# Batch 0's keys in chunks of 128 rows, with one value load each, in an attention and MLP kernel on one core

## The chip, the core and the metric

The kernel runs on one core of a Trainium2 chip. The metric is the device time of one execution in microseconds (us); less is better. Engines: PE (TensorE, matmuls), PEld (its weight loads), DVE (VectorE), ACT (ScalarE), POOL (GpSimd) and SP (SyncE). POOL and SP also issue DMAs.

## The reference

Eight batches, eight heads, 576 positions, head dimension 64; then an MLP on the 4608 tokens, 512 to 2048 to 512.

```python
q_d, k_d, v_d = (means over 4 neighbouring positions of q, k, v)
out_up = repeat(softmax(q_d k_d^T / 8) v_d, 4)            # downsampled attention, 144 x 144
mask = abs(pos[:, None] - pos[None, :]) < 4               # local attention: 7 keys a query
out_local = softmax(where(mask, q k^T / 8, -1e9)) v
x = (out_up + out_local) as [4608, 512]                   # heads side by side
h = x @ w_in
out = (h / (1 + exp(-1.702 h))) @ w_out
```

## The kernel before

The order on each engine is written out by hand: every engine runs its instructions in the order of the program text, and waits where it needs another engine's result. The kernel has a start, in which batch 0's attention is computed, and then nine groups `g` of 512 tokens, each with the two MLP matmuls (`mm1` with `hps_mm`, L764, and `mm2`, L845). The attention of batch `g + 1` is woven into group `g`'s matmuls at fixed places (`POS`, `POS_0`, `VDP_0`).

Local attention: the 576 queries are cut into five chunks `i` at a stride of 114. Before the change a chunk's keys are two runs of 64 (`KSTART`, at 114 i and 114 i + 56) on partitions 0 to 63 and 64 to 127, and each run serves 60 queries (`QSTART`, at 114 i and 114 i + 60). The runs overlap by 8 keys. For batches after the first, `exp_local` and `mask_local` cut out the band with the 0/1 tile `mask`. For batch 0 the band is kept in another way: `bar_others` (L372) first writes -1e6 or 0 into the PSUM tile from `off`, the scores (`scores`, L390) are added, and after the exponential (`exp_apart`, L454) all keys outside the band are zero. It writes to the tiles `ez`, which have 128 columns for each chunk and head; columns that no score reaches are filled once by `fill` (L125, L130, L133). Then `av_local0` (L474) makes one matmul for each chunk and head, with the exponentials as weights and the value tile `vbs[0]` (65 columns, the last one ones, which gives the denominator) as the moving side.

Downsampled attention: the sums of four values are made on PE by `prep_vd_pe` (L355), with a 0/1 selector `psel`, and copied to `vds` by ACT (L362). `scores_d` (L435) and `exp_down` (L461) make the downsampled exponentials `ed`, and `av_down0` (L487) multiplies them with `vds`. `normalise0` (L504 reciprocal, L505 product, DVE) divides both by their denominators into `y`; it is called with chunks 0 to 4 and 4 to 7 for head pairs 0 and 1, and for all seven slots for pairs 2 and 3. `turned` then makes 11 matmuls (`transp_sum`, L525) that turn `y` over and add both kinds, and `copy_x` copies the result to `xT` in three pieces (L536 to L538; ACT, for the last pair partly DVE). The MLP's first matmuls, `part`, read `xT` and `w_in_bf`.

The constants come from iotas on POOL: `dm` (key minus query, for `off` and `mask`), `di` (identity `id128`), `dr` (row number) and `dp` (for `psel`). DVE and ACT turn them into `off`, `id128`, `up` (identity with every column four times), `psel` and `mask` (`make_mask`: ACT's cast L146).

Loads of q, k, v for batches 0 and 1 and of the weights are issued by POOL, with a cast to bf16 on the way: k and q in head groups of four (`load_1`, L201), values as two loads of 64 rows for each chunk (`load_vb`, L232, ten loads a batch), `w_in` in pieces of columns (L255), `w_out` in four pieces (L264). Each POOL load takes the semaphore of the load eight places earlier and so waits until that one has landed. The issue order of the start is:

```python
load_qk(0, 0); load_1("k", k, kf, 0, 1); iota_mask(); load_1("q", q, qf, 0, 1); iota_psel()
fill()
for i in range(5): load_vb(0, i)
load_w_in(0, 512); load_w_in(512, 512); load_w_in(1024, 1024)
```

Dummy matmuls on zeros, `warm`, stand at places where PE would be idle.

Of the kernel before, what the change touches and what calls it, by code (L numbers as in the profile page):

```python
# [8 lines left out]
FP32 = mybir.dt.float32  # L9
# [10 lines left out]
def kernel(  # L20
# [20 lines left out]
    QSTART = (0, 60)  # L41

# [41 lines left out]
    off = consts.tile([128, 60], BF16, name="off")  # L84
    psel = consts.tile([128, 7, 64], BF16, name="psel")
    up = consts.tile([128, 128, 4], BF16, name="up")

    PSEL = [(4, 2), (2, 1), (0, 0), (1, 0), (1, 1), (3, 1), (3, 2)]

    dm = consts.tile([128, 60], FP32, name="dm")  # L90
    di = consts.tile([128, 128], FP32, name="di")
    dr = consts.tile([128, 1], FP32, name="dr")
    bias = consts.tile([128, 4], FP32, name="bias")
    dp = consts.tile([128, 7, 64], FP32, name="dp")
# [3 lines left out]
    def iota_psel():  # L98
        for par in range(2):
            nc.gpsimd.iota(dp[halves[par], 0:3], pattern=[[-72, 3], [-8, 64]],  # L100
                           base=2 * (KSTART[par] + 72) - 3, channel_multiplier=2, **it)
            nc.gpsimd.iota(dp[halves[par], 3:7], pattern=[[72, 2], [-384, 2], [-8, 64]],
                           base=2 * (KSTART[par] + 114) - 3, channel_multiplier=2, **it)

    def iota_mask():
        for par in range(2):
            nc.gpsimd.iota(dm[halves[par]], pattern=[[-1, 60]], base=-4 * par,
                           channel_multiplier=1, **it)
        nc.gpsimd.iota(dr, pattern=[[0, 1]], base=0, channel_multiplier=1, **it)
        nc.gpsimd.iota(di, pattern=[[-1, 128]], base=0, channel_multiplier=1, **it)  # L110

    def fill():
        nc.vector.memset(wz, 0.0)
        nc.vector.memset(ones[:, 0], 1.0)
        nc.vector.memset(ones[:, 1], 4.0)
        for t in kdT:
            nc.vector.memset(t[:, SD:160, :], 0.0)
        for t in vbs:
            nc.vector.memset(t[:, :, :, 64:65], 1.0)
        for t in vds:  # L120
            nc.vector.memset(t[:, :, :, 64:65], 4.0)
        for t in es:
            nc.vector.memset(t[:, :, 300:304], 1.0)
        for t in ez:
            nc.vector.memset(t.rearrange("p j i (x c) -> p (j i x) c", c=64)[:, :, 60:64], 1.0)  # L125
        for n, t in enumerate(ez):
            for par in range(2):
                rest = t[halves[par], :, :, 64 - 64 * par : 124 - 64 * par]
                if n < 2:
                    nc.vector.memset(rest, 0.0)  # L130
                else:
                    zero = wz[halves[par], None, 0:300].to_broadcast([64, 2, 300])
                    nc.scalar.copy(  # L133
                        out=rest, in_=zero.rearrange("p j (i c) -> p j i c", c=60)
                    )


    def make_off():
        nc.vector.tensor_tensor(out=dm, in0=dm, in1=dm, op=ALU.mult)
        nc.vector.tensor_single_scalar(out=dm, in_=dm, scalar=9.5, op=ALU.is_lt)  # L140
        nc.vector.tensor_scalar(
            out=off, in0=dm, scalar1=-1.0, scalar2=1e6, op0=ALU.add, op1=ALU.mult
        )

    def make_mask():
        nc.scalar.copy(  # L146
            out=mask.rearrange("p x (i c) -> p (x i) c", c=60),
            in_=dm[:, None, :].to_broadcast([128, 10, 60]),
        )

    def ident(pos, n, c0, c1):
        return id128[64 * pos : 64 * pos + n, 64 * pos + c0 : 64 * pos + c1]

# [3 lines left out]
    def make_bias():  # L157
        nc.vector.memset(bias[:, 3:4], -3.0)
        nc.vector.tensor_copy(out=bias[:, 0:2], in_=rv)
        nc.vector.tensor_scalar(  # L160
            out=bias[:, 0:2], in0=bias[:, 0:2], scalar1=-1.0, scalar2=400.0,
            op0=ALU.add, op1=ALU.mult,
        )
# [8 lines left out]
    def make_psel():  # L172
        nc.vector.tensor_single_scalar(
            out=rv, in_=dr.to_broadcast([128, 2]), scalar=57.5, op=ALU.is_lt
        )
        nc.vector.tensor_single_scalar(
            out=r2, in_=dr.to_broadcast([128, 2]), scalar=65.5, op=ALU.is_gt
        )
        nc.vector.scalar_tensor_tensor(
            out=r2[:, 0:1], in0=dr, scalar=121.5, in1=r2[:, 0:1],  # L180
            op0=ALU.is_lt, op1=ALU.mult,
        )
        nc.vector.tensor_tensor(out=rv, in0=rv, in1=r2, op=ALU.add)

    def end_psel():
        nc.scalar.activation(out=dp, in_=dp, func=AF.Abs)
        nc.scalar.activation(out=dp, in_=dp, func=AF.Relu, bias=bias[:, 3:4])
        for sl, c in ((slice(0, 1), 1), (slice(1, 7), 0)):
            nc.scalar.activation(
                out=psel[:, sl], in_=dp[:, sl],  # L190
                func=AF.Exp, scale=-400.0, bias=bias[:, c : c + 1],
            )

# [46 lines left out]

    def load_v4(b):
        for kc in range(3):
            for hp in range(HP):
                u, m = hp % 2, hp // 2
                nc.sync.dma_start(
                    out=v4[64 * u : 64 * u + 48, kc, 2 * m : 2 * m + 2],
                    in_=bass.AP(
                        tensor=v.tensor,
                        offset=v[b, 2 * hp].offset + kc * 48 * 4 * D,
                        ap=[[4 * D, 48], [S * D, 2], [1, 4 * D]],  # L250
                    ),
                )
# [21 lines left out]

    def prep_1(name, b, qd):
        store, dst = {"k": (kf, kT), "q": (qf, qT)}[name]
        tt = work.tile([128, S, 2], BF16, name=f"{name}T{qd}", tag=f"{name}T{qd}", bufs=1)
        t32 = tt.rearrange("p t a -> p (t a)").bitcast(FP32)
        nc.vector.transpose(  # L279
            out=t32.rearrange("p (i c) -> p c i", c=18),  # L280
            in_=store[b, qd].bitcast(FP32).rearrange("p (c d) -> p c d", c=18),
        )
        dst[b, qd] = tt
# [10 lines left out]
    def reduce_qk(b, qd, name):  # L294
        t = kdT[qd][:, 0:SD, :] if name == "k" else new_qdT(b, qd)
        src = (kT if name == "k" else qT)[b, qd]
        with nc.allow_low_precision("the sum is rounded once, as the pairwise one is"):
            nc.vector.tensor_reduce(
                out=t, in_=src.rearrange("p (j f) a -> p j a f", f=4),
                axis=mybir.AxisListType.X, op=ALU.add,  # L300
            )

    def pool_qk(b, qd, names="kq"):
        for name, src in (("k", kT), ("q", qT)):
            if name not in names:
                continue
            sv = src[b, qd].rearrange("p (j f) a -> p j f a", f=4)
# [31 lines left out]
    def prep_vd_pe(b, pv, kcs=range(3), between=None):  # L339
        vb, vd = vbs[b % 2], vds[b % 2]  # L340
# [6 lines left out]
        for kc, iis in ((0, (0, 1)), (1, (1, 2, 3)), (2, (3, 4))):  # L347
# [3 lines left out]
            for i in iis:  # L351
                if between:
                    between(kc, i)
                for j in range(2):
                    nc.tensor.matmul(  # L355
                        pv[64 * j : 64 * j + 64, c0 : c0 + D * HP],
                        lhsT=psel[:, PSEL.index((i, kc)), :],
# [12 lines left out]
    def bar_others(sp):  # L370
        for r in range(4):
            nc.tensor.matmul(  # L372
                sp[r // 2][:, r % 2, 0:300],
                lhsT=id128,
                rhs=off[:, None, :].to_broadcast([128, 5, 60]),
# [4 lines left out]
    def scores(b, qd, barred=False, sp=None):  # L380
        if barred:
            bar_others(sp)
        for i in range(5):
            for a in range(2):
                for par in range(2):
                    for r in range(4):
                        rows = slice(32 * r, 32 * r + 32)
                        k0 = 114 * i + KSTART[par]
                        q0 = 114 * i + QSTART[par]
                        nc.tensor.matmul(  # L390
                            sp[r // 2][64 * par : 64 * par + 64, r % 2, 60 * i : 60 * i + 60],
                            lhsT=kT[b, qd][rows, k0 : k0 + 64, a],
                            rhs=qT[b, qd][rows, q0 : q0 + 60, a],
                            start=(a == 0 and not barred),
                            stop=(a == 1 or barred),
                            tile_position=(32 * r, 64 * par),
                            skip_group_check=barred,
# [53 lines left out]
    def exp_apart(qd, sp):  # L451
        for u in range(2):
            for par in range(2):
                nc.scalar.activation(  # L454
                    out=ez[2 * qd + u][halves[par], :, :, 64 * par : 64 * par + 60],
                    in_=sp[u][halves[par], :, 0:300].rearrange("p j (i c) -> p j i c", c=60),
# [53 lines left out]
    def transp_sum(y, x):  # L510
# [9 lines left out]
            (128, i, x[i // 2 % 2][:, c + 3 : c + 117], sub(id128, 3, (61, 2), (1, 57)))  # L520
            for i, c in enumerate((0, 114, 0, 114, 228))
        ]
        turns += [(128, 4, x[0][:, 345:348], id128[:, 121:124])]
# [360 lines left out]
    load_qk(0, 0)  # L884
    load_1("k", k, kf, 0, 1)
    iota_mask()
# [3 lines left out]
    for i in range(5):  # L890
        load_vb(0, i)
    load_w_in(0, 512)
# [6 lines left out]
    warm(14)  # L899
    make_off()  # L900
    make_ident(di)
    make_up()
    make_psel()
    make_bias()
    end_psel()
    prep_1("k", 0, 0)
    prep_1("q", 0, 0)
    sp = scores(0, 0, barred=True, sp=PA[0:2])
# [9 lines left out]
    sp = scores(0, 1, barred=True, sp=PA[0:2])  # L918
    exp_apart(1, sp)
    warm(4, 256)  # L920
    for hp in range(4):
        o[hp] = PB[hp % 3]
        y[hp] = y_tiles0()
    prep_vd_pe(
        0, PM[0], range(0, 2),
        between=lambda kc, i: warm(2 * ((kc, i) == (1, 3)), t=PM[1]),
    )
    for hp in range(2):
        av_local0(hp, o[hp], range(4))
        normalise0(o[hp], y[hp], 0, 4)  # L930
    sd = scores_d(0, 1, PB[2])
    prep_vd_pe(0, PM[1], range(2, 3))
    exp_down(1, sd)
# [5 lines left out]
    make_mask()  # L939

# [16 lines left out]
    normalise0(o[3], y[3])  # L957
    turned(0, None)
# [13 lines left out]
    for g in range(n_groups):  # L972
        b = g + 1
        if g == 0:
# [4 lines left out]
            for qd in range(NQ):  # L979
# [3 lines left out]
                load_qk(2, qd)  # L983
            nc.gpsimd.memset(v4[32:64], 0.0)
# [57 lines left out]
```

## Time and profile before

| | |
|---|---|
| median of 3 runs | 314.41 us (314.29 to 315.14) |
| profiled execution | 316.73 us, its span 314.9 us, granted clock 0.998 |
| PE busy | 300.2 us (95%), 4266 matmuls |
| ACT, DVE, POOL busy | 208.5, 148.3, 151.0 us |
| chain that ended last | PE 86%, DVE 4%, ACT 3%, POOL 2%, DMA 2% |
| first MLP matmul (L764) | at 23.90 us |
| batch 1's value sums (L355) | at 46.58 us |

PE's share of the chain says that the span is the time of PE's work and of what holds it up. Times of single instructions are microseconds from the span's start. Busy PE time is of pipelined matmuls and is not a measure of peak.

### The profile page before, as it was taken

What the parts mean: (1) busy time and instruction counts of PE and PEld (TensorE: products, weight loads), DVE (VectorE), ACT (ScalarE), POOL (GpSimd) and SP (SyncE); (2) the same over time, 40 slices, a digit from 0 to 9 for tenths busy, and PEclk for the clock granted to TensorE, in tenths of its full rate; (3) what the DMA queues carried; (4) which work ended last, traced back from release to release, by engine and by line L of the source; (5) the groups of instructions that cost most, each with busy time, mean ns of one, the idle gap of its engine ahead of it and who ended that gap; (6) DMA issues with size and microseconds to landing.
All of it is one profiled execution on the core that took longest, in us unless ns stands there. A gap on an engine that the chain in (4) does not pass through costs nothing.

```text
span 314.9 us, 9860 instructions
## 1 busy us (share of the span) xinstructions
PE 300.2 (95%) x4266; PEld 161.2 (51%) x4308; DVE 148.3 (47%) x302; ACT 208.5 (66%) x332; POOL 151.0 (48%) x174
## 2 busy tenths in 40 slices
PE   7689999999999999999999999999999999999995
PEld 3467667745554455455545554555455544444444
DVE  7972925790497049803890289027922670000000
ACT  8664875686886688558955895589568857316611
POOL 8852374376336963597339833992397120000000
PEclk9999999999999999999999999999999999999999
DMA  7999999999916980699159914992430110011011
GB/s 120 117 190 211 187 88 194 183 251 232 199 70 173 193 175 36 186 184 200 40 158 191 200 60 134 194 203 76 128 95 5 67 69 0 33 67 35 0 67 67
DMA packets 64123, 39.96 MB, mean 127 GB/s; under 512 B 44624, under 2 KB 54992, under 8 KB 64080
## 3 DMA queue, kind: packets, MB, share of 16 engines
q0 software_dynamic: 18864, 14.95, 35.1%
q1 hardware_dynamic: 45072, 24.32, 30.2%
q8 instruction: 33, 0.54, 0.7%
q14 instruction: 10, 0.08, 0.1%
q10 hardware_dynamic: 144, 0.07, 0.1%
HBM read 44.83 MB, written 9.44 MB: 172 GB/s over the span
## 4 chain that ended last, share of the span: by engine, by line
PE 86%; DVE 4%; ACT 3%; POOL 2%; issue 2%; DMA 2%; DVEq 0%; POOLq 0%; ACTq 0%
PE pm L845 34%; PE pm L764 24%; PE pa L764 15%; PE pa L408 3%; PE pa L654 2%; DMA vb<-in_v_dram 2%; PE pa L632 2%; PE pa L435 2%; DVE y L505 1%; PE pm L860 1%; POOL vb L232 1%; ACT l L600 1%; DVE xT L607 1%; ACT l L589 1%; PE pa L845 1%
## 5 line engine op out<-in xcount | busy, mean ns | idle before, releaser
L845 PE MATMUL pm<-w_out_bf,gT 128*128 128x512 bf16 (+1 forms) x527 | 115.0, 371 | 3.2 <-issue 3.0
L764 PEld LDWEIGHTS <-w_in_bf 128*128 128x128 bf16 x614 | 59.3, 98 | 63.1 <-issue 1.0
L764 PE MATMUL pm<-xT,w_in_bf 128*128 128x512 bf16 (+1 forms) x351 | 87.0, 371 | 0.9 <-ACT osb L828 0.4
L845 PEld LDWEIGHTS <-gT 128*128 128x128 bf16 x604 | 56.9, 98 | 59.7 <-issue 0.7
L775 ACT ACTIVATE gT<-pm 128x512 bf16<-128x512 f32 x88 | 52.7, 604 | 41.0 <-PE pm L764 41.0
L764 PE MATMUL pa<-xT,w_in_bf 128*128 128x512 bf16 (+1 forms) x247 | 59.0, 359 | 0.4
L469 DVE TENSOR_TENSOR es<-es,mask 128x600 bf16<-128x600 bf16 x28 | 17.3, 652 | 88.1 <-ACT es L446 87.9
L828 ACT ACTIVATE osb<-pm 128x512 f32<-128x512 f32 (+2 forms) x35 | 20.3, 582 | 30.5 <-PE pm L845 25.1
L775 ACT ACTIVATE gT<-pa 128x512 bf16<-128x512 f32 x56 | 32.1, 610 | 6.4 <-PE pa L764 6.3
L724 POOL TENSOR_TENSOR xT<-xT,od 128x576 bf16<-128x576 bf16 x12 | 16.7, 1394 | 39.0 <-DVE xT L708 38.7
L708 DVE TENSOR_TENSOR xT<-n,l 128x285 bf16<-128x285 f32 (+1 forms) x96 | 28.2, 368 | 0.0
L310 POOL TENSOR_TENSOR pq<-kT 128x576 f32<-128x576 bf16 x11 | 12.7, 1158 | 30.4 <-DVE kT L279 30.4
L830 DVE TENSOR_SCALAR osb<-pm 128x128 f32<-128x128 f32 x1 | 0.3, 292 | 53.7 <-ACT osb L828 53.7
L327 POOL TENSOR_TENSOR pq<-v 112x512 f32<-112x512 f32 x18 | 23.7, 1316 | 3.2 <-DMA v<-in_v_dram 3.2
L232 POOL DMA_DIRECT2D vb<-in_v_dram x20 | 13.7, 697 | 15.8 <-DMA w_in_bf<-in_moe_w_in_dram 6.9
L279 DVE STREAM_TRANSPOSE kT<-kb 128x576 f32<-128x576 f32 x16 | 20.0, 1249 | 2.5 <-DMA kb<-in_k_dram 2.5
L279 DVE STREAM_TRANSPOSE qT<-qb 128x576 f32<-128x576 f32 x16 | 19.9, 1243 | 0.2 <-DMA qb<-in_q_dram 0.2
L461 ACT ACTIVATE ed<-pa 128x864 bf16<-128x864 f32 x16 | 14.3, 894 | 5.8 <-PE pa L435 5.8
L446 ACT ACTIVATE es<-pa 128x600 bf16<-128x600 f32 x28 | 17.2, 670 | 0.1
L703 ACT ACTIVATE l<-l 128x1440 f32<-128x1440 f32 x12 | 16.8, 1404 | 0.4
L698 DVE COPY n<-pa 128x492 f32<-128x492 f32 x24 | 15.0, 666 | 2.4 <-ACT l L697 1.8
L697 ACT ACTIVATE l<-pa 128x492 f32<-128x492 f32 x24 | 12.6, 578 | 4.3 <-PE pa L654 3.6
(120 smaller groups left out, 363.1 us busy)
## 6 DMA issues: line engine op xcount, KB each, us to landing
out_dram<-osb SPq DMA_DIRECT2D x34, 256.0 KB, 2.1
vf<-in_v_dram SPq DMA_DIRECT2D x60, 128.0 KB, 5.1
v<-in_v_dram SPq DMA_DIRECT2D x72, 96.0 KB, 3.2
kb<-in_k_dram POOLq DMA_DIRECT2D x16, 288.0 KB, 6.5
qb<-in_q_dram POOLq DMA_DIRECT2D x16, 288.0 KB, 8.4
w_out_bf<-in_moe_w_out_dram POOLq DMA_DIRECT2D x4, 512.0 KB, 14.3
vb<-in_v_dram POOLq DMA_DIRECT2D x20, 64.0 KB, 6.1
w_in_bf<-in_moe_w_in_dram POOLq DMA_DIRECT2D x2, 512.0 KB, 8.4
```

The source lines that it names most:

```text
L232: nc.gpsimd.dma_start(out=vbs[b % 2][64 * par : 64 * par + 64, i, :, 0:D], in_=bass.AP(tensor=v.tensor, offset=v[b, 0].offset + (114 * i + ...
L279: nc.vector.transpose(out=t32.rearrange("p (i c) -> p c i", c=18), in_=store[b, qd].bitcast(FP32).rearrange("p (c d) -> p c d", c=18),)
L327: eng.tensor_tensor(out=t1[0:112], in0=x[:, :, 0:2, :], in1=x[:, :, 2:4, :], op=ALU.add)
L446: nc.scalar.activation(out=es[2 * qd + u][:, :, 0:300], in_=sp[u][:, :, 0:300], func=AF.Exp, scale=inv_sqrt_d,)
L469: nc.vector.tensor_tensor(out=ev, in0=ev, in1=mask, op=ALU.mult)
L703: nc.scalar.activation(out=l, in_=l, func=AF.Exp, scale=-1.0)
L708: nc.vector.tensor_tensor(out=out, in0=sub(n, *part), in1=sub(l, *part), op=ALU.mult)
L724: eng.tensor_tensor(out=xs, in0=xs, in1=sub(od[:, u, :], 0, (1, SD), (0, 4)), op=ALU.add)
L764: nc.tensor.matmul(acc[:, c : c + n], lhsT=w_in_bf[:, dmc, ffc * 128 : (ffc + 1) * 128], rhs=xT[dmc][:, g * TG + c : g * TG + c + n], star ...
L775: nc.scalar.activation(out=gT[:, ffc, :], in_=acc, func=AF.Silu, scale=GELU_SCALE)
L828: eng.activation(out=osb, in_=ap, func=AF.Copy, scale=1.0 / GELU_SCALE)
L845: nc.tensor.matmul(ops[t][:, c : c + wide], lhsT=gT[:, ffc, t * 128 : (t + 1) * 128], rhs=w_out_bf[:, ffc, c : c + wide], start=(ffc == 0) ...
```

## The change

For batch 0 a chunk's keys become 128 rows in a row (114 i to 114 i + 127) on partitions 0 to 127. Keys 0 to 63 serve queries 0 to 66 of the chunk and keys 64 to 127 serve queries 61 to 119 (`KEYS0`, `LO0`, `NC0`); a query near the middle has its keys in both halves, in the same column of `ez`. The score tiles get 67 columns for each chunk, and the last chunk gets eight zero keys behind row 576, zero values and a zero in its ones column there. Each chunk has one value load of 128 rows (`load_vb0`; 120 for the last). The selector for the value sums becomes four tiles of 207 columns, of which the matmuls take windows; those of batch 1, which keeps its old chunks, are made on DVE later (`make_psel1`).

The order changes too. The `dr` iota and the band iota for `off` stand ahead of the second k load, `di` ahead of the second q load; the band for `mask` has iotas of its own between two `w_in` loads, and `w_in`'s first 512 columns are two loads of 256. On DVE `off` and the identity are made ahead of the zero fills of `ez`. Head pair 0's AV of chunks 0 to 3 stands ahead of the value sums, and pair 1's behind them. `make_mask` now has two DVE operations, and stands behind the last `normalise0`.

```diff
+    KEYS0, LO0, NC0 = (0, 64), (0, 61), (67, 59)
+    EVEN, ODD = 84, 123
...
     def iota_psel():
+        nc.gpsimd.iota(dp[:, 0:EVEN], pattern=[[-8, EVEN]], base=8 * 18 - 3, channel_multiplier=2, **it)
+        nc.gpsimd.iota(dp[:, EVEN:], pattern=[[-8, ODD]], base=8 * 37 + 4 - 3, channel_multiplier=2, **it)
-        (four iotas on half the partitions)
...
     def fill():
...
+        for t in kT0:
+            nc.vector.memset(t[:, S:, :], 0.0)
+        nc.vector.memset(vbs[0][96:128, 4, :, 0:D], 0.0)
+        make_bias()
+        make_off()
+        make_ident(di)
         (zero fills of ez, now 54 and 62 columns)
...
     def make_mask():
+        nc.vector.tensor_tensor(out=dm, in0=dm, in1=dm, op=ALU.mult)
+        nc.vector.tensor_single_scalar(out=dm, in_=dm, scalar=9.5, op=ALU.is_lt)
         nc.scalar.copy(out=mask..., in_=dm...)
...
+    def make_psel1():
         (four small operations that make rv, as before in make_psel)
+        for c in range(2):
+            for par in range(2):
+                h = halves[par]
+                nc.vector.tensor_scalar(
+                    out=psel[1][c][h, 0:n], in0=psel[0][1][h, 2 * par : n + 2 * par],
+                    scalar1=rv[h, c : c + 1], scalar2=None, op0=ALU.mult)
...
+    def load_vb0(i):
+        n = min(128, S - 114 * i)
+        nc.gpsimd.dma_start(out=vbs[0][0:n, i, :, 0:D],
+            in_=bass.AP(tensor=v.tensor, offset=v[0, 0].offset + 114 * i * D,
+                        ap=[[D, n], [S * D, H], [1, D]]))
...
-                sp[r // 2][:, r % 2, 0:300], ... rhs=off[:, None, :].to_broadcast([128, 5, 60]),
+                sp[r // 2][:, r % 2, 0:335], ... rhs=off[:, None, :].to_broadcast([128, 5, 67]),
...
     load_qk(0, 0)
+    iota_rows()
+    iota_band(dm0, 67, 3)
     load_1("k", k, kf, 0, 1)
-    iota_mask()
+    iota_ident()
     load_1("q", q, qf, 0, 1)
     iota_psel()
     fill()
     for i in range(5):
-        load_vb(0, i)
-    load_w_in(0, 512)
+        load_vb0(i)
+    load_w_in(0, 256)
+    load_w_in(256, 256)
+    iota_band(dm, 60, -4)
     load_w_in(512, 512)
...
-    warm(14)
-    make_off()
-    make_ident(di)
+    warm(12)
+    warm(4, 256)
     make_up()
-    make_psel()
-    make_bias()
-    end_psel()
+    make_psel0()
...
-    prep_vd_pe(0, PM[0], range(0, 2),
-        between=lambda kc, i: warm(2 * ((kc, i) == (1, 3)), t=PM[1]))
-    for hp in range(2):
-        av_local0(hp, o[hp], range(4))
-        normalise0(o[hp], y[hp], 0, 4)
-    sd = scores_d(0, 1, PB[2])
+    def first(hp):
+        av_local0(hp, o[hp], range(4))
+        normalise0(o[hp], y[hp], 0, 4)
+
+    first(0)
+    prep_vd_pe(0, PM[0], range(0, 2))
     prep_vd_pe(0, PM[1], range(2, 3))
-    exp_down(1, sd)
+    first(1)
+    exp_down(1, scores_d(0, 1, PB[2]))
     nc.scalar.preload_act_table_set("silu_and_others")
     for hp in range(3):
         av_local0(hp, o[hp], range(4 if hp < 2 else 0, 5))
         av_down0(hp, o[hp])
         normalise0(o[hp], y[hp], 4 if hp < 2 else 0)
-    make_mask()
...
     av_local0(3, o[3], range(5))
     av_down0(3, o[3])
     normalise0(o[3], y[3])
+    make_mask()
     turned(0, None)
     turned(1, 1)
     part((0, 1), 0)
...
                 reduce_qk(1, qd, "q")
                 load_qk(2, qd)
+            make_psel1()
```

## The prediction

> **What bounds it now.** I read the page's chain by engine first, then the timeline of the first 30 us (the only stretch the change reorders), then the waits of PE's weight loads up to 50 us. The page's chain says that PE carries the span:
>
> ```profile
> PE 86%; DVE 4%; ACT 3%; POOL 2%; issue 2%; DMA 2%; DVEq 0%; POOLq 0%; ACTq 0%
> ```
>
> So what counts is when PE gets its first dense work, the MLP's first matmul, and what waits lie behind it. Timeline, 15.5 to 24 us (start, length, engine, what; the idle time before it in brackets):
>
> ```profile
> 15.93 0.30 PE L355 MATMUL pm<-vb,psel 128*64 128x256 bf16 x2 [0.94 <-DMA vb<-in_v_dram]
> ...
> 16.70 0.11 PEld L355 LDWEIGHTS <-psel 128*64 128x64 bf16 x2 [0.42 <-DMA vb<-in_v_dram]
> ...
> 16.94 0.67 PE L474 MATMUL pa<-vb,l 128*128 128x65 bf16 x16
> ...
> 17.48 0.21 DVE L504 RECIPROCAL rc<-pa 128x8 f32<-128x8 f32 x1 [1.99 <-PE pa L474]
> ...
> 18.78 0.90 ACT L461 ACTIVATE ed<-pa 128x864 bf16<-128x864 f32 x1
> ...
> 19.27 0.20 DVE L504 RECIPROCAL rc<-pa 128x6 f32<-128x6 f32 x1
> ...
> 20.99 0.69 ACT L146 CAST mask<-dm 128x600 bf16<-128x600 f32 x1
> ...
> 22.21 1.09 DVE L505 TENSOR_TENSOR y<-pa,rc 128x896 bf16<-128x896 f32 x1
> ...
> 23.08 0.35 ACT L536 CAST xT<-pm 128x231 bf16<-128x231 f32 x1 [1.41 <-PE pm L525]
> ...
> 23.57 0.28 ACT L538 CAST xT<-pm 128x117 bf16<-128x117 f32 x1
> ...
> 23.90 0.38 PE L764 MATMUL pm<-xT,w_in_bf 128*128 128x512 bf16 x1
> ```
>
> PE waits for values until 16.70; DVE's normalisations then run almost without a gap from 17.48 to 23.30; the MLP starts at 23.90, when ACT has copied the first head pair. The mask cast of 0.69 at 20.99 lies in ACT's idle time. From 23.90 PE has nearly no gap until it needs batch 1's values, where it waits 0.42:
>
> ```profile
> 46.58 0.70 PEld L355 LDWEIGHTS <-psel 128*64 128x64 bf16 x14 [0.42 <-DMA vb<-in_v_dram]
> ```
>
> **Part by part.** *Value loads, ten to five.* Before:
>
> ```profile
> 5.70 4.82 POOL L232 DMA_DIRECT2D vb<-in_v_dram  x7
> 11.45 2.04 POOL L232 DMA_DIRECT2D vb<-in_v_dram  x3 [0.93 <-DMA qb<-in_q_dram]
> ```
>
> Each issue takes 0.69 (4.82/7). The eighth waits 0.93 because a Pool load reuses the semaphore of the load eight places before it, here the last q. The program lists show that five loads keep every value issue clear of that wait. Four fewer iotas go too. A 128-row load is not in the trace: between 0.69 (one half) and 1.39 (two halves); I take 0.9, since 128 rows of k cost 0.56 and the half's 512 pieces 0.69. Values start at about 5.1 and end at 9.6 (8.6 to 12.1) instead of 13.49. But issue is not what PE waits for. The landing records show the sixteen shares of the eighth half: fifteen are in by 15.0 and the last at 16.5; of the fifth, fifteen by 13.4 and the last at 15.3. One DMA engine is late, and the same 5056 pieces (before 5120) pass it. Bounds for chunk 3's landing: 15.0 (the fifteen) to 16.5 (the last); I take 16.5, the row that ends the wait now, and 17.0 for chunk 4 (last half issued at 12.8, shortest landing 4.2).
>
> The Trainium skill, "DMA: Bandwidth & Descriptors", Rules for kernel authors, says that transfers to two partition halves serialise on the same 16 engines and advises one transfer of 128 partitions. By it the change gains issue time and fixed cost; the late share at 16.5 against 15.0 says that issue time is not the limit.
>
> *Constants first.* The dr iota (0.14) and two band iotas (0.2 each) go ahead of k's second load: it lands up to 0.65 later, at 8.9 instead of 8.25, and is needed at 9.56. Covered by 0.66; without cover, 0.65. q's second load is issued at about 4.0 instead of 3.86, and lands at 11.2, needed at 11.85. DVE loses the psel arithmetic (seven small operations from 5.09 to 6.40) but has the 1.54 us of zero fills behind the identity; the first transpose starts at about 6.0 (was 6.17). Gain 0.1, and the exponentials of 630 columns on average instead of 600 cost 4 x 0.03. Net zero. The bars grow by 12% on 0.67 us, 0.08, while PE waits for the transposes anyway.
>
> *Order of AV and value sums.* With chunk 3 at 16.5, head pair 0's last AV ends at about 16.8, and DVE starts at 16.9 (was 17.48). The twelve value-sum matmuls that need chunks 0 to 3 follow, at 0.05 each beside their latency of 0.3, then chunk 4's two, then pair 1's AV until 17.75. ACT copies the sums by 18.15 (0.59 + 0.37), the downsampled scores end at 18.3, exp_down runs 18.35 to 19.25 (was 19.68). Pair 0's rest on DVE starts after its downsampled AV, at about 18.95 (was 19.27). Behind it the same 4.04 of DVE work (19.27 to 23.31): the last normalisation ends at 23.0, a gain of 0.3. Bounds: 22.3 if chunk 4 were in by 15.5, where ACT's exponentials (end 16.75) and copies are late next; 23.3 if nothing is gained. The removed warm(2) was in PE's waiting time.
>
> *The mask.* It no longer sits behind pair 2 but behind the last normalisation: two DVE operations on 128x60 are queued there, and ACT's cast waits for them. **ACT's queue is in order: behind the cast stand all copies of xT, and PE's first MLP matmul waits for the first three.** Rows: 0.22 for the square, 0.28 or 0.78 for the comparison (of these two rows 0.78 is this very operation, beside Pool's iotas; 0.28 is the next one on the same columns; Pool is idle at 22 to 24 us, so 0.28), 0.05 to release ACT, 0.69 cast. 23.0 + 1.24 = 24.24 for the first copy, where before it began at 23.08. The copies take 0.77 and the matmul starts 0.05 later: 25.06 against 23.90, **1.16 us late**. PE's order behind it is the same, and DVE (idle 23.3 to 27.3) loses nothing.
>
> *w_in in pieces.* One more issue of 0.75 on Pool, hidden because the engines are backlogged; rows half as long. Loads with 1024-byte rows ran at about 190 GB/s, 2048-byte rows at 210; by that slope 512-byte rows give about 160, and 524 KB take 0.4 longer (bounds 0 and 0.75). First use is past 24 us, first landings about 19: hidden there. But the whole queue behind it, batch 1's values included, comes 0.4 later. The dm iotas, now between two pieces, cost Pool 0.4 in the same shadow.
>
> *Batch 1's selector* on DVE: four operations of 0.15 to 0.3 and four of about 0.2 behind the last reduction (ends 40.1), before the mask product at 42.15: 1.4 in an idle 2.04. Covered with 0.6 to spare; what exceeded that would hold up the mask product by the excess.
>
> **The sum.** PE would come to batch 1's values at 46.16 (46.58 less its wait) + 1.16 = 47.32; they land at 46.58 + 0.4 = 47.0. PE no longer waits, so 47.32 - 46.58 = **0.74 us** is lost from there on; everything behind follows PE, ACT and DVE in their old distances. The profiled execution had 316.73 us (span 314.9 and 1.8 around it); it becomes 317.47. The median of the runs is 2.32 lower, 314.41, so **315.15 us**. About 0.3% (0.94 us) is what a measurement of this kernel can tell from no change: 313.47 to 315.35 count as the same. Forecast case, 0.4 to 0.94 slower: **0.37**.
>
> **Rivals.**
> - *The gate costs more* (slower). The comparison takes its 0.78 (+0.5), or the queue behind the split w_in comes later than PE by the full 0.75 plus its landing. It decides once the first MLP matmul starts later than 25.25, or batch 1's values land after 47.5. For it: 0.78 is in the trace. Against: Pool's idle time there. Price 0.74 + 0.5 = 1.24, 315.65 (up to 316.2). Chance **0.33**.
> - *PE's clock falls* (slower). PE would have little to do from about 14.5 to 16.5 (two warm-up matmuls fewer) and from about 23 to 25. The first fourteen warm-ups came every 0.43 us (5.76 for 14), later 512-column matmuls every 0.215, so a slow pace exists in this program. Against: idle stretches of 1.2 us before left the pace alone. If the slow pace came back for 3.4 to 5.8 us, half of it is lost: 1.7 to 2.9 more, 316.9 at the near end. Chance **0.07**. The Trainium skill, "TensorE: Matmul & The Clock Gate", Part 1, says that the clock halves after an idle window of about 3.4 us, free-running; by that rule two idle us mostly pass, and no window here is idle throughout.
> - *The late share vanishes* (same). Chunk 4 in by 15.5: normalisations end at 22.3, the first matmul at 24.36, 0.46 late, which the 0.42 absorbs: 314.4 to 314.8. Chance **0.10**.
> - *Faster.* Values in by 15, and the last normalisation off the gate: if the comparison and cast overlap the normalisation, PE starts with the transposes of pair 0, which now end in a PE gap of 0.8 (21.93 to 22.73, nothing shown that it waits for). Without that gap and with values earlier: start at 23.05, 0.85 early; batch 1's values would have to come 1.3 earlier as well, which ends 1.3 below, 313.1. For it: the value stream has thin stretches (61 GB/s at 15 to 16 us) that five early issues could fill. Against: the program's order puts the cast behind both DVE operations. Chance **0.13**.
>
> **How the numbers follow.** Faster 0.13; same 0.37 + 0.10 = 0.47; slower 0.33 + 0.07 = 0.40. The forecast case itself holds 314.8 to 315.35. The range goes down to 313.4, which leaves out about half of the faster case, and up to 316.5, which leaves out the clock case and the last of the costlier gate: about 0.15 in all.
>
> **What would show it.** In the changed profile: five value issues without a wait for a q load; DVE's first reciprocal near 16.9; ACT's mask cast beginning after the last normalisation, near 23.5, named as waiting for DVE; the first MLP matmul on PE near 25.0; no wait of the batch 1 value sums for a DMA, near 47.3. The forecast is wrong if the cast ends before pair 0's transposes, if values land before 15.5 and the MLP starts before 23.9, if batch 1's value sums start before 46.5, or if PE's matmuls of 512 columns come more than 0.22 apart after 25 us.

## The result and the profile after

| | before | after |
|---|---|---|
| median, us | 314.77 (314.29 to 315.87, 4 runs) | 318.07 (317.76 to 318.56, 4 runs) |
| ratio | | 1.0101, 95% interval 1.007 to 1.0133 |
| profiled execution, us | 316.73, span 314.9 | 318.13, span 316.4 |
| mean granted clock of the profiled execution | 0.998 | 0.993 (0.992 or 0.993 in all four runs) |
| first MLP matmul, us | 23.90 | 24.89 |

The kernel became 1.0% slower, 3.3 us. The prediction had said 315.15 with a range up to 316.5. The granted clock of every run is given in what follows, because some kernels here have two groups of times that can't be understood without it.

The timeline of the changed kernel (start, length, engine, what; in brackets the idle time before it and what ended it):

```profile
4.80 4.51 POOL L268 DMA_DIRECT2D vb<-in_v_dram  x5
...
16.28 0.25 PE L514 MATMUL pa<-vb,l 128*128 128x65 bf16 x3 [1.84 <-issue]
...
16.64 0.21 DVE L544 RECIPROCAL rc<-pa 128x8 f32<-128x8 f32 x1 [1.45 <-ACT l L493]
...
18.53 0.89 ACT L501 ACTIVATE ed<-pa 128x864 bf16<-128x864 f32 x1 [0.41 <-PE pa L474]
...
18.98 0.20 DVE L544 RECIPROCAL rc<-pa 128x6 f32<-128x6 f32 x1
...
21.96 1.09 DVE L545 TENSOR_TENSOR y<-pa,rc 128x896 bf16<-128x896 f32 x1
...
22.20 0.32 PE L565 MATMUL pm<-id,y 128*128 128x114 bf16 x4 [0.50 <-issue]
...
23.21 0.19 DVE L164 TENSOR_SCALAR dm<-dm 128x60 f32<-128x60 f32 x1
...
23.49 0.69 ACT L165 CAST mask<-dm 128x600 bf16<-128x600 f32 x1 [2.77 <-DVE dm L164]
...
24.09 0.35 ACT L576 CAST xT<-pm 128x231 bf16<-128x231 f32 x1
...
24.57 0.27 ACT L578 CAST xT<-pm 128x117 bf16<-128x117 f32 x1
...
24.89 0.88 PE L804 MATMUL pm<-xT,w_in_bf 128*128 128x512 bf16 x2 [1.61 <-ACT xT L578]
...
48.82 0.70 PEld L396 LDWEIGHTS <-psel 128*64 128x64 bf16 x14 [0.42 <-issue]
```

Two things are to be seen. ACT stands idle for 2.77 us, then makes the mask at 23.49, and only then the three copies for which PE waits 1.61 us. And the first two MLP matmuls of 512 columns take 0.88 together, where an execution of the kernel before, shown further down (b_look2), has two in 0.59. The granted clock says why. Windows of the changed kernel (length, busy time of PE, PEld, DVE, ACT and POOL with their instructions, then granted clock, DMA share and GB/s):

```profile
22.00:24.00 2.00, 1.09 (x15) 0.86 (x15) 1.37 (x3) 0.51 (x1) 0.70 (x1) 1.00 1.12 213
24.00:26.00 2.00, 1.11 (x5) 0.46 (x4) 0.00 (x0) 1.51 (x7) 0.00 (x0) 0.77 1.16 222
26.00:30.00 4.00, 4.00 (x34) 2.88 (x34) 0.16 (x1) 1.12 (x4) 1.65 (x3) 0.69 1.09 206
```

PE has about half its time idle from 22 to 26, and the clock falls to half just as its dense work begins; in the clock records it is at half from 25.06 to 28.48. The page's chain by engine has more of PE than before, since a slow PE is still a busy one:

```profile
PE 92%; DVE 5%; issue 1%; ACT 1%; ACTq 0%; DVEq 0%
```

### The profile page after: what moved, and what is told of

It is laid out like the page before. It is cut to its first block, busy times and chain, and to the rows that moved or that the text cites. A ratio compares the mean times of both kernels' runs of the same rounds, so it can differ in the third digit from the quotient of the medians.

```text
span 316.4 us, 9906 instructions
## 1 busy us (share of the span) xinstructions
PE 304.6 (96%) x4308; PEld 162.1 (51%) x4308; DVE 148.8 (47%) x311; ACT 207.9 (66%) x332; POOL 148.5 (47%) x170
## 4 chain that ended last, share of the span: by engine, by line
PE 92%; DVE 5%; issue 1%; ACT 1%; ACTq 0%; DVEq 0%
PE pm L885 36%; PE pm L804 25%; PE pa L804 15%; PE pa L447 3%; PE pa L885 2%; PE pa L694 2%; PE pa L474 2%; PE pa L672 2%; DVE y L545 1%; PE pm L900 1%; DVE kT L320 1%; PE pa L565 1%; PE pa L607 1%; PE pa L595 0%; DVE qT L320 0%
## 5 line engine op out<-in xcount | busy, mean ns | idle before, releaser
L885 PE MATMUL pm<-w_out_bf,gT 128*128 128x512 bf16 (+1 forms) x550 | 119.5, 371 | 0.0
L804 PE MATMUL pm<-xT,w_in_bf 128*128 128x512 bf16 (+1 forms) x366 | 89.7, 373 | 1.6 <-ACT xT L578 1.6
L737 ACT ACTIVATE l<-pa 128x492 f32<-128x492 f32 x24 | 12.6, 578 | 4.6 <-PE pa L694 3.7
L447 PE MATMUL pa<-qT,kT 32*64 32x60 bf16 x1120 | 15.3, 195 | 0.0
```

What stands on the lines that cost most here:

```text
L447: nc.tensor.matmul(P[1 + r // 2][64 * par : 64 * par + 64, r % 2, 60 * i : 60 * i + 60], lhsT=kT[b, qd][rows, k0 : k0 + 64, a], rhs=qT[b, ...
L804: nc.tensor.matmul(acc[:, c : c + n], lhsT=w_in_bf[:, dmc, ffc * 128 : (ffc + 1) * 128], rhs=xT[dmc][:, g * TG + c : g * TG + c + n], star ...
L885: nc.tensor.matmul(ops[t][:, c : c + wide], lhsT=gT[:, ffc, t * 128 : (t + 1) * 128], rhs=w_out_bf[:, ffc, c : c + wide], start=(ffc == 0) ...
```

## The experiments

Names: `a_` kernels start from the changed one, `b_` kernels from the one before. "Full clock" means a run whose mean granted clock is 0.997 or more. By arithmetic one half-clock stretch of 3.4 us in some 314 makes the mean about 0.994, and three make it about 0.984.

**b_again: the kernel before, unchanged.** It tells how typical the profiled execution was that the prediction was summed against.

> The kernel before, unchanged, run again beside itself. It gives the spread that a difference has to exceed, and a second profile: the one at hand (316.73 us) lies 2 us above the timed runs (314.3 to 315.9). Gate-and-clock theory: no slow clock between 5 and 310 us, MLP start near 23.9 us, ratio 1.000 within 0.003. Rival (the kernel before has two tempos and the loss is partly a matter of which one was met): spans of its runs differ by 2 us or more.

Measured: 314.79 us median, 12 runs of 313.98 to 316.69; ratio 0.9983 (0.9958 to 1.0009). The profiled one, 316.69, was the slowest of the twelve. So executions of one binary lie 2.7 us apart, and both profiles of before at hand were at the upper edge. In this one the first MLP matmul comes at 22.95, without the stall of 0.8 in pair 0's transposes. It loses time later, where DVE and POOL add at the same moment:

```profile
53.51 1.98 DVE L607 TENSOR_TENSOR xT<-n,l 128x285 bf16<-128x285 f32 x4
...
53.97 1.42 POOL L618 TENSOR_TENSOR xT<-xT,od 128x576 bf16<-128x576 bf16 x1
```

The four DVE additions took 0.96 together three us earlier (at 50.38), where POOL was idle.

**b_look2: before once more, one execution.**

> The kernel before once more, for a third profile. Baseline theory (the profile that the prediction summed against holds delays that most executions do not have): the first MLP matmul near 22.9 us without a gap in pair 0's transposes, the gate cast of POOL on w_out's last piece near 50.5 instead of 54.0, and 314 to 315.5 us. Rival (a profiled execution of this kernel is always 2 us longer): 316.5 to 317 again.

Measured: 314.10 us, span 312.3. Its timeline:

```profile
21.35 0.35 ACT L536 CAST xT<-pm 128x231 bf16<-128x231 f32 x1 [0.41 <-PE pm L525]
...
22.17 0.59 PE L764 MATMUL pm<-xT,w_in_bf 128*128 128x512 bf16 x2
...
50.04 0.40 POOL L881 CAST vf<-w_out_bf 1x1 f32<-1x1 bf16 x1 [3.26 <-DMA w_out_bf<-in_moe_w_out_dram]
...
52.45 0.31 DVE L607 TENSOR_TENSOR od<-n,l 128x144 f32<-128x144 f32 x1 [0.80 <-ACT l L600]
```

and the same work in the profile that the prediction used:

```profile
54.01 0.18 POOL L881 CAST vf<-w_out_bf 1x1 f32<-1x1 bf16 x1 [4.41 <-DMA w_out_bf<-in_moe_w_out_dram]
...
54.16 1.20 POOL L618 TENSOR_TENSOR xT<-xT,od 128x576 bf16<-128x576 bf16 x1
54.19 1.35 DVE L607 TENSOR_TENSOR od<-n,l 128x144 f32<-128x144 f32 x1 [0.80 <-ACT l L600]
```

The MLP starts at 22.17, not 23.90 (1.73 of the 2.63 us between the two executions). The rest, 0.90, lies behind: in the slower one POOL's cast waited for `w_out` until 54.01, its addition then started beside DVE's, and DVE's took 1.35 instead of 0.31. What follows: the profiled execution held 2.63 us of stalls that this one has not. That its distance of 2.32 us to the median was such stalls is read from this one pair; b_look2 itself lies 0.3 to 0.8 under the medians of before.

**a_mask_last: the changed kernel, mask behind the last transposes.**

```diff
     normalise0(o[3], y[3])
-    make_mask()
     turned(0, None)
...
     turned(3, 0)
+    make_mask()
     part((2, 3), 1)
```

> The changed kernel with the mask's two DVE operations and its cast moved behind the copies of the last head pair; all else as changed. Gate-and-clock theory: ACT's first copy starts near 22.6 us instead of 24.09, the first MLP matmul near 23.3 instead of 24.89, no stretch of half clock at 25 to 28.5 us, and the time falls by about 3 us from 318.1 to 315 or a little below the kernel before (314.2 to 315.2). Rival (the loss is in the new order of AV and value sums, the loads or batch 1's selector): at least 317.

Measured: 315.49 us (314.53 to 318.51, 12 runs), ratio 1.0028 (1.0006 to 1.005). The profile, span 313.4, clock 1.0:

```profile
21.93 0.32 PE L565 MATMUL pm<-id,y 128*128 128x114 bf16 x4 [0.68 <-issue]
...
22.29 0.35 ACT L576 CAST xT<-pm 128x231 bf16<-128x231 f32 x1 [2.01 <-PE pm L565]
...
23.10 0.38 PE L804 MATMUL pm<-xT,w_in_bf 128*128 128x512 bf16 x1
```

Moving one call gives back 2.6 of the 3.3 us: the first copy comes 1.80 earlier, the MLP 1.79. The median lies a little above the forecast 314.2 to 315.2. Of the twelve runs six had the full clock (median 314.95, level with the 314.87 of before's runs beside them) and six 0.984 to 0.994 (315.35 to 318.51). PE's gap of 0.68 inside pair 0's transposes, with nothing shown that it waits for, is still there.

**a_warm_gate: the changed kernel, PE kept busy while the gate is closed.**

```diff
     turned(1, 1)
+    warm(7, t=PB[2][:, 0, :])
     part((0, 1), 0)
```

> The changed kernel with seven dummy matmuls of 512 columns (1.5 us of PE) between the second pair's transposes and the first MLP matmul, where PE waits for the copies; the mask stays where the change put it. Gate-and-clock theory: the MLP still starts near 24.9 us, but at full clock; of the 3.3 us only the late start of 1.0 us is left: 315.3 to 316.5. If the clock had no part: 318 as the changed kernel.

Measured: 316.92 us (315.79 to 319.42, 8 runs), ratio 1.0078 (1.005 to 1.0106). Seven runs had the full clock (median 316.87); the one at 0.993 took 319.42. The MLP starts at 25.13, no earlier than in the changed kernel, and the run is still 1.2 us shorter; behind the last dummy matmul PE still waits 0.31 for ACT's copies. So the fallen clock is 1.2 us of the loss. The forecast for this kernel, 315.3 to 316.5, was missed by 0.4: it took the gate at 1.0. What the gate costs with the clock kept is this kernel against a_mask_last, both at full clock: 316.87 - 314.95 = 1.9 us.

**b_gate: the kernel before, with the gate alone.**

```diff
+    dm2 = consts.tile([128, 60], FP32, name="dm2")
...
     def make_mask():
+        nc.vector.tensor_tensor(out=dm2, in0=dm, in1=dm, op=ALU.mult)
+        nc.vector.tensor_single_scalar(out=dm2, in_=dm2, scalar=0.5, op=ALU.is_gt)
         nc.scalar.copy(out=mask..., in_=dm2...)
...
-    make_mask()
...
     normalise0(o[3], y[3])
+    make_mask()
```

> The kernel before with the gate alone: two DVE operations on 128x60 behind the last normalisation, from whose result ACT casts the mask ahead of the copies of xT. Nothing else of the change. Gate-and-clock theory: the MLP starts near 25.4 us (23.30 + 0.45 + 0.69 + 0.77 + 0.1), PE is idle some 2 us and the clock is halved for 3.4 us: 317.5 to 319. If the clock keeps: 315.5 to 316. Rival (the gate is harmless): 314.8.

Measured: 317.66 us (315.95 to 319.32, 6 runs), ratio 1.0083 (1.0051 to 1.0115). The profile is of the 315.96 run:

```profile
22.95 0.69 ACT L149 CAST mask<-dm 128x600 bf16<-128x600 f32 x1 [2.72 <-DVE dm L148]
...
24.36 0.38 PE L767 MATMUL pm<-xT,w_in_bf 128*128 128x512 bf16 x1 [2.28 <-ACT xT L541]
```

The same picture in a kernel with none of the other edits, and the clock splits the runs cleanly: 315.95 and 315.96 at 0.998 and 0.999; 317.57, 317.74 and 318.14 at 0.993 and 0.994; 319.32 at 0.988. A half-clock stretch costs 1.6 to 2.2 us here, near half of 3.4; in a_mask_last the five runs at 0.993 or 0.994 are 0.4 to 2.1 above the full-clock median, so the price depends on what the stretch meets. The gate is enough to make before nearly as slow as the changed kernel. Two things are unlike the pair above. The two full-clock runs are only 1.1 us above the 314.87 of before's runs beside them. And the MLP starts at 24.36, not at the forecast 25.4, which was added up from rows of the slow profile of before.

**b_gate_warm: b_gate with dummy matmuls in the wait.**

```diff
     turned(1, 1)
+    warm(8, t=PB[2][:, 0, :])
     part((0, 1), 0)
```

> The kernel before with the gate alone, as in the run above, and eight dummy matmuls of 512 columns in PE's wait for the copies. Gate-and-clock theory: the two groups of times that the gate alone gave (315.95 and 317.6 to 319.3) become one near 316, 1.3 to 1.9 us above the kernel before, with no stretch of half clock. Rival (the upper group has another cause): two groups again.

Measured: 316.23 us (316.09 to 317.65, 6 runs), ratio 1.0063 (1.0042 to 1.0083). All six runs are at 0.997 or more, where four of b_gate's six were not; the warm-ups hold the clock. Two are still near 317.65. The profile of one (317.64, clock 1.0) has batch 0's values late, first normalisation at 17.36; its span is only 314.9, though, so 2.7 us lie outside the span where other runs have some 1.8. Against before beside it, 314.35, the gate without any clock loss costs 1.9 us, as in the first pair, where b_gate's two full-clock runs gave 1.1.

**a_ml_order: a_mask_last with the old order of AV and value sums** (and the `warm(2)` that belonged to it).

```diff
+    prep_vd_pe(0, PM[0], range(0, 2),
+        between=lambda kc, i: warm(2 * ((kc, i) == (1, 3)), t=PM[1]))
     first(0)
-    prep_vd_pe(0, PM[0], range(0, 2))
-    prep_vd_pe(0, PM[1], range(2, 3))
     first(1)
-    exp_down(1, scores_d(0, 1, PB[2]))
+    sd = scores_d(0, 1, PB[2])
+    prep_vd_pe(0, PM[1], range(2, 3))
+    exp_down(1, sd)
```

> The changed kernel with the mask behind the copies (as in the run before this) and with the old order of AV and value sums, two warm-up matmuls included. Order theory (the 0.6 us that this kernel still lost with the mask out of the way come from pair 1's AV standing behind chunk 4's sums): about 314.8, level with the kernel before. Load theory (they come from the loads): 315.5, no change. The first normalisation should start 0.3 us later than 16.4, the second right behind it without a gap.

Measured: 314.98 us (313.95 to 315.30, 12 runs), ratio 1.0006 (0.9996 to 1.0017): level with before by the ratio, though its median is 0.4 above the 314.56 of before's runs beside it. The first normalisation starts at 17.34, later than the forecast 16.7. All twelve runs are at full clock, six of a_mask_last's were not; at full clock the two are equal (314.98 and 314.95). The new order costs nothing by its own length. It makes PE idle early: in the emptiest 3.41 us from 10 us on PE is busy for 1.82 in a_mask_last (12.6 to 16.0) and for 2.22 here.

**a_ml_avboth: a_mask_last with both pairs' first AV ahead of the value sums.**

```diff
     first(0)
+    first(1)
     prep_vd_pe(0, PM[0], range(0, 2))
     prep_vd_pe(0, PM[1], range(2, 3))
-    first(1)
```

> The changed kernel with the mask behind the copies and with both pairs' first AV ahead of all value sums. Order theory: DVE's second normalisation follows the first without the gap of 0.3 us, but the value sums and so ACT's copies come 0.35 later: 315.2 to 315.6, within 0.3 us of the run with the mask moved alone. If it is faster than the kernel before by 0.3 us or more, pair 1's place was the loss.

Measured: 315.02 us (314.64 to 318.01, 12 runs), ratio 1.0025 (1.0004 to 1.0046); nine runs at full clock, median 314.94, a little under the forecast 315.2 to 315.6. Pair 1's normalisation moves from 17.63 to 17.21, and the first MLP matmul stays (23.09 for 23.10), because PE's gap in pair 0's transposes is 0.82 here. The gap ends at the same time in both, 21.92 and 21.93.

**a_ml_halves: a_mask_last with ten value loads of 64 rows.**

```diff
-        nc.gpsimd.dma_start(out=vbs[0][0:n, i, :, 0:D], in_=(n rows))
+        for r0, r1 in ((0, 64), (64, n)):
+            nc.gpsimd.dma_start(out=vbs[0][r0:r1, i, :, 0:D], in_=(rows r0 to r1))
```

> The changed kernel with the mask behind the copies and each value chunk loaded as two loads of 64 rows again (ten loads). Load theory (the early 128-row loads push back PE's instruction packets, from 11.9 to 13.1-13.4 us for the first and with it the second, which leaves PE a gap of 0.5 to 0.7 us in pair 0's transposes): the first packet near 11.9, no such gap, 314.8. Order theory: 315.5 as with the mask moved alone, or worse by the later issue of the last chunks.

Measured: 315.69 us (314.0 to 320.38, 12 runs), ratio 1.0037 (1.0008 to 1.0066). Seven runs at full clock, median 314.87; five at 0.976 to 0.993, 316.79 to 320.38. The profiled run, 318.25, had the clock at half from 17.89 to 28.13, three stretches. Its PE waits for values twice in the AV (0.62 and 1.31) and is busy for 1.48 of the 3.41 us from 13.2. PE's gap in pair 0's transposes is gone, as the load theory said, but the kernel is not faster for it.

**a_ml_halves_warm: the same with six warm-ups ahead of the first AV.**

```diff
+    warm(6)
     def first(hp):
```

> The changed kernel with the mask behind the copies, ten value loads, and six dummy matmuls of 512 columns ahead of the first AV, where PE waits for values. Clock theory (the upper group of the run without them, 316.3 to 320.4, is the clock that falls in that wait): one group, 314.0 to 315.1, and level with or 0.2 us below the kernel before (314.6). Rival (ten loads make late values and nothing else): the upper group stays.

Measured: 315.96 us (315.18 to 316.38, 7 runs), ratio 1.0044 (1.0029 to 1.0059). All seven at full clock, as the clock theory said, but at 315.96 and not at the 314.0 to 315.1 of six of a_ml_halves' seven full-clock runs: a miss by 0.9. Warm-ups hold the clock. That the missing time is theirs is not shown: in the profile (316.38) the MLP starts at 23.17, level with a_mask_last's 23.10, and what it loses comes at 53.70, where DVE's four additions beside one of POOL take 1.98 instead of 0.96, as in b_again.

**a_ml_order_halves: a_ml_halves in the old order.** The same diff as a_ml_order. What is left of the change are the contiguous keys, the order of the constants, the split `w_in` and batch 1's selector.

> The changed kernel with the mask behind the copies, ten value loads and the old order of AV and value sums: of the change only the key chunks of 128 rows, the constants ahead of the loads, the w_in pieces and batch 1's selector are left. If these cost nothing, as predicted: 314.3 to 314.8, level with the kernel before. If the split of w_in or the selector costs 0.4: 315.

Measured: 315.25 us (314.39 to 318.92, 12 runs), ratio 1.004 (1.0013 to 1.0067). The ten runs at full clock have a median of 315.09, two at 0.984 took 318.72 and 318.92. It was expected at 314.3 to 314.8, also a miss. The edits that are left bring nothing that shows; at full clock the kernel is 0.7 above the 314.35 of before's runs beside it, and which of them costs this was not tested. In its profile the MLP starts early, at 22.34, and the addition of DVE at 52.64, beside POOL's, takes 0.87 instead of 0.31.

**a_ml_warm: a_mask_last with six warm-ups ahead of the first AV.** The same diff as a_ml_halves_warm.

> The kernel after with the mask moved behind the last transposes, and six warm-up matmuls (about 1.3 us) ahead of head pair 0's first AV, where PE waited 1.59 us for chunk 3's values. Of the mask-moved kernel's twelve runs six had the clock granted in full (0.997 and more; median 314.95) and six a mean of 0.984 to 0.995 (315.35 to 318.51); its median was 315.49. Clock theory: what is left of the change's cost once the gate is gone is PE's thin stretch at 14 to 16 us, which in half the executions brings the half clock back. Then with the warm-ups at least ten of twelve runs are at 0.997 or more, the median is 314.7 to 315.2, and PE's gap of 0.5 to 0.8 in pair 0's transposes may stay. Rival, the order or the 128-row loads cost time by themselves (late values, late instruction packets): the clock is full and the median stays at 315.4 to 316.0, as the warm-ups removed nothing from that chain. Second rival: the warm-ups do not help, the clock still falls in about half the runs, median 315.5.

Measured: 315.99 us (315.55 to 319.42, 12 runs), ratio 1.0056 (1.0032 to 1.008). Ten of twelve at full clock, but their median is 315.94. The clock part of the theory holds and its time is missed by 0.7. The number is that of the first rival (315.4 to 316.0, the order or the 128-row loads cost time by themselves); against its reason stand a_mask_last's own full-clock runs at 314.95, with the same order and loads. The timeline shows more than was asked for:

```profile
13.65 1.69 PE L771 MATMUL pm<-wz 128*128 128x256 bf16 x8
...
16.29 0.38 PE L771 MATMUL pm<-wz 128*128 128x512 bf16 x1 [0.94 <-issue]
```

The last of six dummy matmuls on zeros, which needs no value and writes the same tile as the five before it, stops for 0.94 us and comes at 16.29. So PE's stop near 16 us in the changed kernel is not only a wait for values. The DMA records show 16 KB packets of an instruction queue in each profile. In the changed kernel the first came at 13.39 and took 1.56, and PE went on at 16.28. All gaps of PE over 0.2 us marked "issue" between 12 and 26 us, fourteen in nine kernels, end 1.25 to 1.61 us after such a packet's end. That PE waits for its next instructions there is read from this regularity; the five other profiles have such packets too and no such gap, so a packet alone does not stop PE. The first packet starts at 12.89 to 13.39 in the six kernels with 128-row loads and at 11.54 to 12.33 in the eight profiles with 64-row loads. Why it starts later there was not found.

All kernels by clock:

| kernel | runs | median, all | at full clock | median of those |
|---|---|---|---|---|
| b_again | 12 | 314.79 | 12 | 314.79 |
| after | 4 | 318.07 | 0 | |
| a_warm_gate | 8 | 316.92 | 7 | 316.87 |
| a_mask_last | 12 | 315.49 | 6 | 314.95 |
| a_ml_order | 12 | 314.98 | 12 | 314.98 |
| a_ml_avboth | 12 | 315.02 | 9 | 314.94 |
| a_ml_halves | 12 | 315.69 | 7 | 314.87 |
| a_ml_halves_warm | 7 | 315.96 | 7 | 315.96 |
| a_ml_order_halves | 12 | 315.25 | 10 | 315.09 |
| a_ml_warm | 12 | 315.99 | 10 | 315.94 |
| b_gate | 6 | 317.66 | 2 | 315.95 |
| b_gate_warm | 6 | 316.23 | 6 | 316.23 |

The kernel before took 314.35 to 314.87 beside them (medians of 17 to 29 runs, all but one of 89 at full clock). None of these versions beats it.

## Why the prediction was wrong

The sum had 1.16 for the gate, 0.42 of slack taken off it, and nothing for PE's clock. Measured were 1.9 for the gate, no slack, and 1.2 to 1.3 for the clock, together nearly all of the 3.3. What else the change costs at full clock is 0.1 in a_mask_last (314.95, before beside it 314.87) and 0.3 to 0.7 in the versions with ten loads, the old order or another order, each against before's runs beside it; only the 0.7, of a_ml_order_halves, is clear of the runs' scatter, and it was not explained. The prediction had the gate as its forecast and got its place on the timeline right, but not its price; the clock it had as a rival at 0.07.

- **Start and values: right in time, not in reason.** First reciprocal 16.9 forecast, 16.64 seen; pair 0's rest 18.95 and 18.98; exp_down 18.35 and 18.53; five value issues from 4.80 without a wait, at 0.90 each. But "Bounds for chunk 3's landing" took the landing as the only limit. Chunk 3 landed at 16.09, and PE's stop, which ends at 16.28, is marked "issue". The matmul that it stops at is the sixth, of chunk 2, whose values had landed at 13.79. So the forecast time came by luck: a stop that it did not know of ended close to the landing that it reckoned with.
- **The gate's place: right.** Last normalisation ends at 23.05 (23.0), the cast starts at 23.49 (23.5), the MLP at 24.89 (25.06).
- **The gate's price: the step "25.06 against 23.90, 1.16 us late" failed.** The gated start was nearly right (24.89); the row it was set against was not a usual one. The 23.90 came from an execution in which PE had stalled 0.80 inside pair 0's transposes, the gap that the faster rival names, and the gate hides such a stall. The other two profiles of before start the MLP at 22.95 and 22.17, and a_mask_last at 23.10, so that 24.89 is 1.94, 2.72 and 1.79 late. At full clock two pairs of kernels measured 1.9, and b_gate's two full-clock runs 1.1. Adding the stall back, 1.16 + 0.80 = 1.96, comes near the 1.9, but in part by chance: a_mask_last has a gap of 0.68 there itself. Carrying the "2.32 lower" over to the changed kernel had the same fault: the offset was stalls of that execution (the start 1.73 late, the POOL and DVE meeting 0.90, against b_look2), and the gate keeps the start late in every run.
- **The absorbed 0.42, "PE no longer waits": wrong.** The 0.42 at batch 1's values was the idle time of PEld, the weight loads. The line at 48.82 after has the same 0.42 with "issue" as its end, and so have b_look2 (44.84) and a_mask_last (45.79); b_again has 0.42 too (45.65), with the DMA named. PE's matmuls had no idle time before them there in before either. There was no slack to absorb anything.
- **The clock rival: right in mechanism, far too small a chance, and the sum put the clock at nothing.** It forecast 1.7 to 2.9 more and 1.2 to 1.3 came. From its first MLP matmul on, with the 1.8 us outside the span, the changed kernel took 318.13 - 24.89 = 293.24, b_look2 314.10 - 22.17 = 291.93. Against the rival had stood "idle stretches of 1.2 us before left the pace alone". What mattered was not the single gap but PE's busy time in a fixed window.

  In the clock records of all fourteen profiles every change lies a whole number of 3.413 us behind the moment when the clock first became full (after: 4.58, 25.06, 28.48; a_ml_halves: 4.23, 17.89, 28.13). Cut on that grid, the window ahead of the fall holds 1.30 us of PE work in the changed kernel (first line) and 1.63 in a_ml_halves (second line):

```profile
21.65:25.06 3.41, 1.30 (x17) 0.96 (x16) 1.68 (x5) 1.57 (x6) 0.70 (x1) 1.00 1.12 212
...
14.47:17.89 3.42, 1.63 (x26) 1.27 (x26) 1.55 (x3) 2.42 (x4) 3.35 (x8) 1.00 1.36 146
```

  No full-clock window with 1.70 or more, in any profile, was followed by a fall; one with 1.46, where a_ml_halves ends, was not either. So by the profile's busy times the limit lies near half a window; it is not settled closer. The grid lies differently in each execution, which makes it a matter of chance. In b_gate's profile PE is busy for only 1.07 in the emptiest 3.41 us (21.4 to 24.8), but the grid cuts that stretch in two, and the clock stayed full:

```profile
19.78:23.19 3.41, 2.29 (x44) 1.80 (x44) 3.04 (x7) 0.69 (x2) 0.59 (x2) 1.00 1.17 214
23.19:26.61 3.42, 2.20 (x20) 1.48 (x20) 0.00 (x0) 2.54 (x10) 0.13 (x1) 1.00 1.12 213
```

  Four of b_gate's six runs fell, all four of the changed kernel, five of a_ml_halves' twelve and one of a_warm_gate's eight (1.34 near 15 us). Why a_mask_last, with 1.82 in its emptiest 3.41 us from 10 us on, fell in six of twelve its one profile does not show.

  The Trainium skill, "TensorE: Matmul & The Clock Gate", Part 1, tells of a free-running window of about 3.4 us and of results that vary with its phase. The trace agrees on both (the grid of 3.413 us, and b_gate's runs at four different clocks). It gives an idle window as the condition; here a window with 1.30 us of work in it, and no gap over 1.61, was enough.
- **The split of `w_in`, "0.4 later": not seen.** By its own rates (524 KB at 160 and 190 GB/s) the term should have been 0.5. The last three value loads of batch 1 are issued at 38.15 after, at 38.40 in b_look2, and nothing waits for them.
- **Faster: no.** "Without that gap" was half of that rival. The gap stays with 128-row loads in all but one of the profiles with the gate open, and where it is gone (a_ml_order, a_ml_halves) the time is level with before.

What stays open: why the instruction packet starts later with 128-row loads, how many of the timed runs have the meeting of DVE and POOL at 54 us, which only a profile shows, why the clock stayed at half for three windows in a_ml_halves and for one in the changed kernel, and where the 0.7 us of a_ml_order_halves go.

## What to carry to other kernels

A cast that waits for another engine belongs behind the copies that feed the bottleneck engine, not ahead of them: in an in-order queue its wait becomes theirs. Before summing against one profiled execution, see where its time lies among the timed runs, and take its accidental stalls (a gap with no releaser, two engines that met by chance) out of the row that the sum is made against, because a new wait hides them and does not add to them. An idle time of PEld is not one of PE, and when a change thins out PE's work, count its busy time in stretches of 3.4 us, wherever they may begin; where one holds less than about half, give the half clock a chance and a price (0.4 to 2.2 us for one stretch here).

## What was not expected of the hardware

- The clock fell to half after windows in which PE was busy for 1.30 and 1.63 of 3.41 us, and every change of it lay on a grid of 3.413 us (fourteen profiles). It stayed at half for 3.42 us in the changed kernel (mean clock 0.993) and for 10.24, three windows, in a_ml_halves (0.984).
- A DVE operation of 0.31 us took 1.35 when a POOL tensor operation of 1.20 started beside it; four of 0.96 together took 1.98 beside one of 1.42 (b_again).
- PE can stop for 0.3 to 1.8 us on a matmul that lacks no data that the profile shows, and goes on 1.25 to 1.61 us after a 16 KB packet of instructions has come in over the DMA engines; such a packet took 0.9 to 2.1 us while the loads ran.
- Two executions of one binary differ by up to 2.7 us in 314 at full clock; between two of them it was when the first MLP matmul came (1.73) and whether POOL and DVE met (0.90).
